# Turning the small matrices of two linear-attention layers by DMA instead of rebuilding them on TensorE

## The chip, the core and the metric

The kernel runs on one core of a Trainium2 chip, in one launch. A core has five instruction streams that matter here: TensorE (PE in the profile; its weight loads are PEld), VectorE (DVE), ScalarE (ACT), GpSimd (POOL) and SyncE (SP), which issues every DMA of this kernel in one queue. The metric is the device time of the core in microseconds; a comparison uses the median of several runs.

## The reference, cut to what matters

Forward and backward pass of four residual layers on x of 2048 tokens by 512 features, bfloat16. Layers 0 and 2 are linear attention with the same weights, layers 1 and 3 gated linear units with the same weights. The outputs are the forward result and the gradients of x and of the five weight matrices.

```
phi = lambda t: jnp.where(t > 0, t + 1, jnp.exp(t)) + 1e-6
pq, pk = phi(q), phi(k)                              # 32 heads of 16
kv = jnp.einsum("bhsd,bhse->bhde", pk, v)            # per head 16x16
z = jnp.einsum("bhsd->bhd", pk)                      # sum of the keys
o = (pq @ kv) / (pq @ z + 1e-6);  return o @ wo
...
x = x + A(layernorm(x)); x = x + B(layernorm(x))     # layers 0, 1
x = x + A(layernorm(x)); x = x + B(layernorm(x))     # layers 2, 3
out, vjp = jax.vjp(f, x, wqkv, wo, w_gate, w_up, w_down)
```

An attention layer thus passes through a few small matrices that every token depends on: kv (128x512 as four block-diagonal 128x128 blocks), z, and kv times wo, called Wp (512x512). The backward pass needs the same things turned, and its own: the gradient of kv (dkv) and its products with the value weights, U and its transpose UT.

## The kernel before, in words

Tokens are worked in eight blocks of 256, each as two halves of 128. Five sweeps go over the blocks, and neighbouring sweeps overlap:

- sweep 1: layernorm of layer 0, keys (`a_k`, k_ps) and the sum G of h times pk (g_acc, g_ps), queries (`a_q`, q_ps);
- first barrier (`a_barrier` of layer 0): kv from G (kv_ps), Wp from kv (wp_ps), z;
- sweep 2: attention output of layer 0 (`a_p2`: den_ps, reciprocal, ya_ps), layernorm, layer 1 (g_ps, u_ps, y_acc of `glu_fwd`), layernorm, keys and queries of layer 2;
- second barrier (`a_barrier` of layer 2);
- sweep 3: attention output of layer 2, layer 3 forward and backward (`glu_both`), and the first half of layer 2's backward pass (`a_b1`: dpn_ps with WpT and Zn, m_ps);
- backward barrier (`a_bbarrier`): dkvT, U (u_ps), UT, dkv;
- sweep 4: the second half of layer 2's backward pass (`a_b2`: dpk_ps with U, dha_ps with UT), layer 1 backward, first half of layer 0's;
- sweep 5: the rest of layer 0, and then `dw`: the weight gradients (dw_ps), which fill the last quarter.

No instruction order is written out by hand. Each function adds pieces to a plan `k.G` (class `Plan`): a piece has a key such as `UT2.1`, its time on TensorE, the keys it follows, the engine steps behind it with their costs, and the buffer tokens it takes and gives. `Plan.run` plays an event model with one queue for each engine and one for DMA ("D"), and issues the instructions in the order in which the model grants them. A piece's rank is the longest path behind it plus an entry of the table `OFFSETS`. On the chip each engine keeps that order, so that an instruction that waits holds all behind it on its engine; SP does so with DMAs too. Model costs decide the order alone, not the time on the chip. Transfers are modelled as megabytes over a rate: `RATE` for plain ones, `TURNED` for DMA transposes.

What the change touches:

- In `a_barrier`, `wpt` computes Wp turned a second time from kv and wo (L739, 16 matmuls of 128 columns for each layer), and `turn` makes kv and Zn (z in blocks, turned) by four TensorE transposes each (L759). Results go from PSUM to SBUF by ACT. Layer 0's WpT is stored to WpT_d and loaded again as WpTl in sweep 4.
- In `a_bbarrier`, `ut` computes UT (L1102, four matmuls of 512 columns for each layer) and `dkv` the untransposed dkv from MTb and woT (L1111, 16 matmuls), beside `dkvT` (L1069) and `u` (L1079).
- In `a_k`, `zsum` adds up the keys (L642): 16 matmuls of one column for every two blocks, into z_ps, for both layers.
- Turns by DMA exist already: rTx from rx in `a_p2` (L861), gT from g in `a_b1` (L1009), both 128x512 from SBUF, and larger ones from HBM (hT, pkT, the dw_sets).

Pools: PSUM has five "mm" buffers, two "acc" and one "tp"; SBUF has six "s1" buffers of 128x512 and seven "w4" of 512x512.

Of the kernel before, what the change touches and what calls it, by code (L numbers as in the profile page):

```python
# [74 lines left out]
class Plan:  # L75
# [11 lines left out]
    RATE, TURNED = 0.27, 0.235  # L87
# [16 lines left out]

    def load(self, key, fn, mb, deps=(), use="", pull=0.0, turn=False):
        self.add(key, fn, 0.0, deps, [("D", mb / (self.TURNED if turn else self.RATE))], use, pull=pull)

    def store(self, key, fn, mb, deps=(), free=""):
        self.add(key, fn, 0.0, deps, [("D", mb / self.RATE, free)], side=True)
# [169 lines left out]
TURN = (6, 1, 1)  # L279
ACCJ, ACCY = 11, 7  # L280
# [8 lines left out]
    DE0:3=-33,4=+11,5=+6,7=+11 DE2:0=-23,1=-155,2=-22 DK0:4=+21 DP0:0=+49,1=-15,2=+49,3=+49,4=-66,7=-5  # L289
    DP2:2=+21,4=+10,5=+30 DT0:+79 DW1:1=-22,2=-1,3=-1,5=-8,6=-49,7=-9 DW3:1=+10,4=-2 E3:0=+1,1=-1 Fg3:11=+20  # L290
    G1:0=-32,1=+1 G11:1=+46,5=-36,6=+40 GS0:3=+14,4=-9,5=-66,6=-362 GS2:6=+63 J1:0=+63 K0:0=-17,2=+93 K2:2=+31
    LB1:2=-23 LB2:7=+3 LB3:2=-24,4=+2 LDH2:6=-3 LDL0:7=+15 LDP0:3=-7,7=-7 LDX0:4=-6 LG3:0=+67
    LN0:1=-208,2=-119,5=-109,6=-19,7=-144 LN2:7=-83 LP2:1=+18 LS1:3=-4,5=-4,6=-4 LX0:3=+16,4=+16 MS0:1=-1,5=-128
    MS2:1=-29 Q0:1=-86,4=-160,6=-53,7=+154 Q2:0=-18,1=-11,2=-12,4=+2 RX2:2=+53,3=-30 S0:-40 SDX1:4=-62 SDX3:0=-92
    SH2:2=-17,4=-11 SHH1:2=-21,4=-21,5=-92 SJ1:+26 SM2:-84 SN0:4=+85,5=-2 SO0:3=-11 SP2:2=-92,3=+50 SPREAD:-142
    SQ0:1=-58 SR0:3=-38,4=-57,5=-38,6=-36,7=-38 SU1:0=-17,6=-41 SU3:2=-14 TG0:1=+2,2=+6,4=-73 TK0:2=+394,5=+132
    TR1:2=+19,5=-7 TR3:4=+32 WT2:0=+41,1=+12 Y1:4=-9 Y33:1=-27,4=-34 YA0:0=-98,6=+10 YA2:1=-31,2=+11 ZE0:3=+36,5=-31
    ZE2:0=+58,1=+61,2=+78,3=+94,4=+173,5=+131,6=+174 ZN2:-46 ZS0:3=+12 ZS2:7=+79 ZZ2:-116
# [7 lines left out]
def kernel(  # L306
# [48 lines left out]
    k.WpT_d = dt_("WpT_d", [P, NDC * D])  # L355
# [69 lines left out]
def build_consts(k, consts):  # L425
# [33 lines left out]
    k.pm = consts.tile([P, 2], F32, name="pm")  # L459
# [51 lines left out]

def layernorm(k, l, b, x_fn, deps, sums=False):
# [4 lines left out]
    def half_sums(j):  # L517
        if j == 0:
            k.h[l, b] = t2(k, f"h{l}", [P, 2, D])
        h, x_t = k.h[l, b], x_fn()  # L520
        col = slice(2 * B + j, 2 * B + j + 1)
        rs, sx = k.rstd[l][:, col], k.sx[l][:, 2 * b + j:2 * b + j + 1]
        q = k.p1.tile([P, 4], F32, name="ln_q", tag="ln_q", bufs=4)
        nc.scalar.activation(h[:, j, :], x_t[:, j, :], ACT.Square, accum_out=q[:, 0:1])
        yield
        nc.gpsimd.tensor_tensor(q[:, 1:3], sx.to_broadcast([P, 2]), k.pm[:], ALU.mult)
        yield
        nc.gpsimd.tensor_scalar(q[:, 0:1], q[:, 0:1], 1.0 / D, EPS_LN, ALU.mult, ALU.add)
        yield
        nc.gpsimd.tensor_scalar(rs, q[:, 1:2], q[:, 2:3], q[:, 0:1], ALU.mult, ALU.add)  # L530
        yield
        nc.gpsimd.tensor_tensor(rs, rs, k.neghalf[:, 0:1], ALU.pow)
        yield
        nc.gpsimd.tensor_tensor(q[:, 3:4], q[:, 1:2], rs, ALU.mult)
        yield
        nc.scalar.activation(h[:, j, :], x_t[:, j, :], ACT.Identity, bias=q[:, 3:4], scale=rs)
        if l in k.rstdh:
            yield
            nc.gpsimd.tensor_scalar(k.rstdh[l][:, col], rs, 0.5, 0.0, ALU.mult, ALU.add)
# [46 lines left out]
def a_k(k, l, b, keep, by_dma=False):  # L586
# [50 lines left out]
    def zsum():  # L637
        ps = tpps(k, [P, NDC], "z_ps", F32)
        for c in range(NDC):
            for i in range(4):  # L640
                bb, j = b - 1 + i // 2, i % 2
                nc.tensor.matmul(ps[:, c:c + 1], lhsT=A.pk[bb][:, j, cslice(c)], rhs=k.ones_col[:],  # L642
                                 start=(i == 0), stop=(i == 3))
        yield
        if b == 1:
            A.z = k.p1.tile([P, NDC], F32, name="z", tag="z", bufs=2)
            nc.vector.tensor_copy(A.z[:], ps[:])
        else:
            nc.vector.tensor_tensor(A.z[:], ps[:], A.z[:], ALU.add)
# [7 lines left out]
    if l == 2 and b in SUMS:  # L657
        gs, prev = SUMS[b]
        for m in range(NDC):
            G.add(f"GS{n}.{m}", lambda m=m: gsum(m, gs, True, True), 2 * len(gs) * C512,  # L660
                  [f"K{l}.{bb}.{j}" for bb in gs for j in range(2)] + [f"GS{l}.{prev}.{m}"] + ([f"<GS{n}.{m - 1}"] if m else []),
                  [("A", 0.59, "-mm") if b == 1 else ("V", 0.69, "-mm")],
                  "+mm" + (" +accf" if b == 1 and m == 0 else " +w4" if b == NBLK - 1 and m == 0 else ""))
    if b % 2 == 1:
        bs = [b - 1, b]
        ks = [f"K{l}.{bb}.{j}" for bb in bs for j in range(2)]
        G.add(f"ZS{n}", zsum, 16 * 0.027, ks + [f"ZS{l}.{b - 2}", f"ZB{l - 2}"], [("V", 0.2, "-tp")], "+tp")
        for bb in bs:
            nb = b if l == 2 and bb not in SUMS else bb
            G.free("-t2", [f"<GS{l}.{nb}.3", f"SH{l}.{bb}", f"TK{l}.{bb}.1"])  # L670
            G.free("-t2", [f"<GS{l}.{nb}.3", f"SPK{l}.{bb}", f"<ZS{n}"])
# [13 lines left out]
def a_barrier(k, l):  # L685
# [42 lines left out]
    G.add(f"KV{l}", kv, 16 * C128, cg + ["WV", f"KT{l - 2}", f"WT{l - 2}.3", f"ZN{l - 2}"], [("V", 0.69, "-mm")], "+mm")  # L728
# [4 lines left out]

    def wpt(m):
        if m == 0:
            A.WpT = w4(k, f"WpT{l}")
        ps = mmps(k, [P, NDC, P], "wpt_ps")
        for c in range(NDC):
            nc.tensor.matmul(ps[:, c, :], lhsT=k.wo[:, c, cslice(m)], rhs=A.kvT[:, c, :], start=True, stop=True)  # L739
        yield  # L740
        nc.scalar.copy(A.WpT[:, m, :], flat(ps[:]))
# [11 lines left out]
    def turn(nm):  # L753
        src = st["zbd"] if nm == "Zn" else A.kvT[:]
        dst = k.consts.tile([P, NDC, P], BF16, name=f"{nm}{l}")
        setattr(A, nm, dst)
        tps = tpps(k, [P, NDC, P], "zn_ps")
        for c in range(NDC):
            nc.tensor.transpose(tps[:, c, :], src[:, c, :], k.ident[:])  # L759
        yield  # L760
        nc.scalar.copy(dst[:], tps[:])
    for m in range(NDC):
        G.add(f"WT{l}.{m}", lambda m=m: wpt(m), 4 * C128, wps + ([f"<WT{l}.{m - 1}"] if m else []), [("A", 0.59, "-mm")],
              "+mm" if m else "+mm +w4")
    if l == 0:
        G.store("SW", lambda: nc.sync.dma_start(out=k.WpT_d[:], in_=flat(A.WpT[:])), 2 * BLK, [f"WT{l}.{m}" for m in range(NDC)], "-w4")
    G.add(f"ZB{l}", zbd, 0.0, [f"ZS{l}.{last}"] + wps, [("V", 0.68, "+s1"), ("V", 0.17)])
    G.add(f"ZN{l}", lambda: turn("Zn"), 4 * C128, [f"ZB{l}"], [("A", 0.59, "-tp")], "+tp -s1")
    G.add(f"KT{l}", lambda: turn("kv"), 4 * C128, wps, [("A", 0.59, "-tp")], "+tp")
# [172 lines left out]
def a_b1(k, l, b, deps):  # L942
# [71 lines left out]
    for hf in range(2):  # L1014
        G.add(f"DP{n}.{hf}", lambda hf=hf: dpn(hf), 8 * C256,
              [f"TG{n}.0", f"TG{n}.1"] + ([f"LP{n}", "WPL0"] if l == 0 else [f"LP{n}"]) + ([f"<DP{n}.0"] if hf else [f"<DP{l}.{b - 1}.1"]) + [f"WT{l}.{m}" for m in range(NDC)],
# [39 lines left out]
def a_bbarrier(k, l):  # L1056
# [41 lines left out]
    def ut(c):  # L1098
        if c == 0:
            A.UT = w4(k, f"UT{l}")  # L1100
        ps = mmps(k, [P, D], "ut_ps")
        nc.tensor.matmul(ps[:], lhsT=st["dkvT"][:, c, :], rhs=k.wvT[:, c, :], start=True, stop=True)  # L1102
        yield
        cp(k, c, A.UT[:, c, :], ps[:])

    def dkv():
        A.dkv = k.consts.tile([P, NDC, P], BF16, name=f"dkv{l}")
        ps = mmps(k, [P, NDC, P], "dkv_ps")
        for c in range(NDC):
            for m in range(NDC):  # L1110
                nc.tensor.matmul(ps[:, c, :], lhsT=A.MTb[:, m, cslice(c)], rhs=k.woT[:, m, cslice(c)],  # L1111
                                 start=(m == 0), stop=(m == NDC - 1))
        yield
        nc.vector.tensor_tensor(A.dkv[:], ps[:], bdm(), ALU.mult)
# [8 lines left out]
    for c in range(NDC):  # L1123
        G.add(f"UT{l}.{c}", lambda c=c: ut(c), C512, [f"<U{l}.3"] + ([f"<UT{l}.{c - 1}"] if c else []), cpost(c, "mm"),
              "+mm" if c else "+mm +w4")
    G.add(f"DKV{l}", dkv, 16 * C128, [f"<U{l}.3"] + ms, [("V", 0.69, "-mm")], "+mm")
    G.free("-w4", [f"SM{l}", f"<DKV{l}", f"<DT{l}"])
    G.free("-s1", [f"<U{l}.3", f"<UT{l}.3"])
# [454 lines left out]
def sweep1(k):  # L1583
# [9 lines left out]
    for b in range(NBLK):  # L1593
# [5 lines left out]
        a_k(k, 0, b, True)  # L1599
# [8 lines left out]
    G.free("-w4", ["<WT2.3", "<WP2.3"])  # L1608
# [3 lines left out]
def sweep2(k):  # L1612
# [26 lines left out]
    G.free("-w4", [f"<YA0.{last}.1"])  # L1639
# [3 lines left out]
def sweep3(k):  # L1643
# [35 lines left out]
    G.free("-w4", [f"<YA2.{last}.1"])  # L1679
# [6 lines left out]
def sweep4(k):  # L1686
# [4 lines left out]
    def wpl():  # L1691
        A0.WpT = w4(k, "WpTl")
        nc.sync.dma_start(out=flat(A0.WpT[:]), in_=k.WpT_d[:])
# [3 lines left out]
    G.load("WPL0", wpl, 2 * BLK, [f"<DP2.{last}.1", "WKT", "SW", "UT2.3"], "+w4")  # L1697
# [17 lines left out]
    G.free("-w4 -w4", ["<UT0.3", "<DKV0"])  # L1715
# [220 lines left out]
```

## Time and profile before

| | |
|---|---|
| runs | median 1094.3 us of 9 (1092.81 to 1096.01) |
| profiled execution | 1092.81 us, its span 1091.0 us |
| matmuls | 7524 |
| DMA | 236.94 MB in 491745 packets, mean 217 GB/s |
| busy share, DVE / ACT / POOL | 59% / 33% / 16% |
| DMA issues | all on SP, one after another |

The span runs from the first to the last instruction; the profiled execution's time has 1.8 us around it. A row's "busy" is the union of the times of its instructions, and matmuls overlap, so that a row's mean is longer than the distance from one matmul to the next. "Idle before" is what the engine waited ahead of an instruction, with what ended the wait. For a DMA, the row on SPq is the time of the issue; the landing comes later.

### The profile page before, as it was taken

The numbers are of one execution on the slowest core, as the hardware profiler recorded it, in microseconds if no ns is written. First come the engines' busy times: TensorE is split into PE (matmuls) and PEld (weight loads), VectorE is DVE, ScalarE is ACT, GpSimd is POOL, SyncE is SP. The second block draws the span as 40 slices with busy tenths as digits, with TensorE's granted clock in tenths as the row PEclk, the third lists the DMA queues.
The fourth block names the chain that finished last, engine by engine and source line by source line (L and its number), as shares of the span: only waits on it lengthen the run. The fifth ranks groups of instructions, "written<-read, shape, count | busy, mean of one in ns | idle before, by whom it ended". The sixth has DMA issues, their size and how long they took to land.

```text
span 1091.0 us, 19982 instructions
## 1 busy us (share of the span) xinstructions
PE 1068.9 (98%) x7524; PEld 700.7 (64%) x7524; DVE 640.2 (59%) x1580; ACT 363.6 (33%) x729; POOL 172.3 (16%) x444
## 2 busy tenths in 40 slices
PE   6989999999999999999999999989999999999998
PEld 3667767667567666676556566656554466666787
DVE  6897776699766886788856667868746000000010
ACT  6675565456343343332244543332111000000010
POOL 4136655305230212000000000000000000000000
PEclk9999999999999999999999999999999999999999
DMA  7748889984988888765979699969999999999960
GB/s 239 246 128 282 233 253 270 280 187 130 227 215 214 207 220 198 203 160 136 277 202 259 210 274 255 273 153 261 238 252 278 239 224 205 232 227 223 198 157 20
DMA packets 491745, 236.94 MB, mean 217 GB/s; under 512 B 317600, under 2 KB 476544, under 8 KB 489600
## 3 DMA queue, kind: packets, MB, share of 16 engines
q1 hardware_dynamic: 491648, 235.66, 85.0%
q8 instruction: 59, 0.97, 0.4%
q14 instruction: 38, 0.31, 0.1%
HBM read 62.46 MB, written 95.72 MB: 145 GB/s over the span
## 4 chain that ended last, share of the span: by engine, by line
PE 74%; DVE 2%; SPq 1%; DMA 1%; issue 0%; ACT 0%; DVEq 0%; ACTq 0%
PE dw_ps L1818 26%; PE dha_ps L1205 8%; PE dh_acc L1336 7%; PE dh_acc L1334 7%; PE dhh_ps L1264 7%; PE g_ps L1264 3%; PE u_ps L1264 3%; PE y_ps L1456 3%; PE dpk_ps L1189 3%; PE m_ps L1036 2%; PE dpn_ps L975 2%; PE ya_ps L901 1%; DMA dw_set<-hh_d 1%; PE gT_ps L483 1%; PE dpn_ps L988 1%; PE q_ps L790 1%
## 5 line engine op out<-in xcount | busy, mean ns | idle before, releaser
L1818 PE MATMUL dw_ps<-dw_set,h 128*128 128x352 bf16 (+2 forms) x1536 | 205.6, 297 | 0.0
L1818 PEld LDWEIGHTS <-h 128*128 128x128 bf16 x1536 | 150.3, 98 | 55.3
L1800 DVE TENSOR_SCALAR dw_o<-dw_ps 128x512 bf16<-128x512 f32 (+3 forms) x33 | 17.6, 540 | 232.0 <-PE dw_ps L1818 226.7
L1336 PE MATMUL dh_acc<-wgT,dg 128*128 128x512 bf16 x352 | 133.4, 379 | 0.2 <-DVE dg L1511 0.2
L1334 PE MATMUL dh_acc<-wuT,du 128*128 128x512 bf16 x352 | 133.4, 379 | 0.0
L1798 ACT ACTIVATE dw_o<-dw_ps 128x512 bf16<-128x512 f32 (+4 forms) x34 | 16.1, 481 | 245.2 <-PE dw_ps L1818 229.7
L1264 PE MATMUL u_ps<-hT,wu 128*128 128x256 bf16 x704 | 92.5, 273 | 0.0
L1264 PE MATMUL g_ps<-hT,wg 128*128 128x256 bf16 x704 | 92.5, 273 | 0.0
L1264 PE MATMUL dhh_ps<-gT,wdT 128*128 128x256 bf16 x704 | 88.4, 273 | 1.3 <-ACT gT L485 1.2
L1143 POOL TENSOR_SCALAR ab<-c 128x2 f32<-128x2 f32 x64 | 20.2, 316 | 410.0 <-DVE lnb_j L1140 409.5
L1264 PEld LDWEIGHTS <-wg 128*128 128x128 bf16 x704 | 68.5, 98 | 21.3
L1818 PE MATMUL dw_ps<-g,dw_set 128*128 128x512 bf16 (+1 forms) x352 | 77.9, 379 | 2.9 <-DMA dw_set<-hh_d 2.9
L1264 PEld LDWEIGHTS <-wdT 128*128 128x128 bf16 x704 | 68.4, 98 | 14.4 <-issue 2.0
L1264 PEld LDWEIGHTS <-wu 128*128 128x128 bf16 x704 | 68.9, 98 | 8.0
L1818 PEld LDWEIGHTS <-dw_set 128*128 128x128 bf16 (+1 forms) x352 | 35.1, 100 | 42.1 <-DMA dw_set<-hh_d 3.4
L1137 ACT ACTIVATE lnb_t<-dha_ps,rstd 128x512 f32<-128x512 f32 x32 | 22.0, 687 | 109.2 <-PE dha_ps L1205 79.0
L1336 PEld LDWEIGHTS <-dg 128*128 128x128 bf16 x352 | 34.4, 98 | 35.1 <-DVE dg L1511 0.5
L1334 PEld LDWEIGHTS <-du 128*128 128x128 bf16 x352 | 34.4, 98 | 34.4
L1389 ACT ACTIVATE th<-g_ps 128x512 f32<-128x512 f32 (+1 forms) x48 | 26.7, 557 | 73.7 <-PE g_ps L1264 54.6
L1295 DVE SCALAR_TENSOR_TENSOR hh<-th,u_ps 128x512 bf16<-128x512 f32 (+1 forms) x48 | 30.3, 638 | 24.2 <-ACT th L1290 17.2
L1509 DVE TENSOR_TENSOR du<-s2tl,dhh 128x512 bf16<-128x512 bf16 (+1 forms) x48 | 18.9, 401 | 41.1 <-ACT dhh L1504 38.3
L1306 PE MATMUL y_acc<-wd,hh 128*128 128x512 bf16 x176 | 42.7, 379 | 0.0
(215 smaller groups left out, 1821.1 us busy)
## 6 DMA issues: line engine op xcount, KB each, us to landing
s2t_d<-s2t SPq DMA_DIRECT2D x8, 1408.0 KB, 6.1
s2tl<-s2t_d SPq DMA_DIRECT2D x8, 1408.0 KB, 7.7
hh_d<-hh SPq DMA_DIRECT2D x16, 640.0 KB, 4.5
du_d<-du SPq DMA_DIRECT2D x80, 128.0 KB, 2.8
dg_d<-dg SPq DMA_DIRECT2D x80, 128.0 KB, 2.9
h_d<-h SPq DMA_DIRECT2D x32, 256.0 KB, 2.6
h<-h_d SPq DMA_DIRECT2D x18, 256.0 KB, 4.4
pk_d<-pk SPq DMA_DIRECT2D x16, 256.0 KB, 3.1
```

What stands on the lines that cost most here:

```text
L975: nc.tensor.matmul(ps[:, c2, :], lhsT=A.WpT[:, m, cslice(c)], rhs=st["gT"](m), start=(c2 + m == 0), stop=False, skip_group_check=True)
L1137: nc.scalar.activation(t[:], dh_ps, ACT.Identity, scale=rs, accum_out=c12[:, 0:1])
L1189: nc.tensor.matmul(ps[:, c2, :], lhsT=A.U[:, m, cslice(2 * hf + c2)], rhs=st["hT"][:, m, :], start=(m == 0), stop=(m == NDC - 1))
L1205: nc.tensor.matmul(ps[:], lhsT=lh[:, c, tslice(j)], rhs=rh[:, c, :], start=(i + c == 0), stop=(i == 2 and c == NDC - 1))
L1264: nc.tensor.matmul(ps[:, i, :], lhsT=w[:, m, fsl(fc)], rhs=rhsT[:, m, :], start=(m == 0), stop=(m == NDC - 1))
L1295: nc.vector.scalar_tensor_tensor(hh, th[:, 0:w], 1.0, flat(up[:])[:, 0:w], ALU.add, ALU.mult)
L1306: nc.tensor.matmul(st["acc"][j][:], lhsT=st["hh"][:, fc, tslice(j)], rhs=k.wd[:, fc, :], start=(fc == 0), stop=(fc == NFC - 1))
L1334: nc.tensor.matmul(acc[j][:], lhsT=du[:, i, tslice(j)], rhs=k.wuT[:, fc, :], start=(fc == 0), stop=False)
L1336: nc.tensor.matmul(acc[j][:], lhsT=dg[:, i, tslice(j)], rhs=k.wgT[:, fc, :], start=False, stop=(fc == NFC - 1))
L1389: nc.scalar.activation(th[:, 0:w], flat(gp[:])[:, 0:w], ACT.Tanh, scale=0.5)
L1456: nc.tensor.matmul(ps[:], lhsT=st["hh"][:, fc, tslice(j)], rhs=k.wd[:, fc, :], start=(fc == 0), stop=(fc == NFC - 1))
L1818: nc.tensor.matmul(ps, lhsT=lhs(s_), rhs=rhs(s_), start=(s_ == 0), stop=(s_ == 31))
```

## The change

- `add_dma_turn` is new: it turns a 512x512 matrix by four DMA transposes of 128x512, SBUF to SBUF. Layer 2's WpT comes from Wp this way, and UT from U in both layers. `wpt` and `ut` are gone.
- Zn, kv and dkv are turned by one DMA transpose each. The TensorE transposes and the dkv matmuls are gone.
- Layer 0's Wp is stored as it is (Wp_d) and turned as it is loaded in sweep 4 (WpTl).
- In layer 2, blocks 0 to 6 of the keys are added up by GpSimd into zf (fp32, one copy and 13 adds of 128x512). At the end `zsum` sums zf over its rows with four fp32 matmuls against a column of ones (k.pm) and adds block 7 with eight bfloat16 matmuls. Layer 0 keeps its 64 matmuls.
- The event model has a faster plain rate with a floor for each issue, and two rates for turned transfers, split at 0.3 MB. `OFFSETS` has new values, so the order changes in many places. `TURN0 = 8` adds an argument that is false for every block.

```diff
-    RATE, TURNED = 0.27, 0.235
+    RATE, ISSUE, TURNED, SETS = 0.3, 0.45, 0.225, 0.22
...
+    def moved(self, mb, turn=False):
+        if turn:
+            return mb / (self.SETS if mb > 0.3 else self.TURNED)
+        return max(mb / self.RATE, self.ISSUE)
...
+def add_dma_turn(k, key, get, make, deps, use="", free=""):
+    st = {}
+    def turn(i):
+        if i == 0:
+            st["t"] = make()
+        k.nc.sync.dma_start_transpose(out=st["t"][:, :, cslice(i)], in_=get(i))
+    for i in range(NDC):
+        k.G.load(f"{key}.{i}", lambda i=i: turn(i), BLK, deps[i] + ([f"~{key}.{i - 1}"] if i else []), "" if i else use, turn=True)
...
+    def zadd(j):
+        pk = A.pk[b][:, j, :]
+        if j == 0 and b == 0:
+            A.zf = k.p1.tile([P, D], F32, name=f"zf{l}", tag="lnf", bufs=BUFS["lnf"])
+            nc.gpsimd.tensor_copy(A.zf[:], pk)
+        else:
+            nc.gpsimd.tensor_tensor(A.zf[:], A.zf[:], pk, ALU.add)
...
         for c in range(NDC):
-            for i in range(4):
-                bb, j = b - 1 + i // 2, i % 2
-                nc.tensor.matmul(ps[:, c:c + 1], lhsT=A.pk[bb][:, j, cslice(c)], rhs=k.ones_col[:],
-                                 start=(i == 0), stop=(i == 3))
+            if l == 2:
+                nc.tensor.matmul(ps[:, c:c + 1], lhsT=A.zf[:, cslice(c)], rhs=k.pm[:, 2:3], start=True, stop=False)
+            for i, t in enumerate(its):
+                nc.tensor.matmul(ps[:, c:c + 1], lhsT=t[:, cslice(c)], rhs=k.ones_col[:],
+                                 start=(l == 0 and i == 0), stop=(i == len(its) - 1))
...
-            nc.tensor.matmul(ps[:, c, :], lhsT=k.wo[:, c, cslice(m)], rhs=A.kvT[:, c, :], start=True, stop=True)
-        nc.scalar.copy(A.WpT[:, m, :], flat(ps[:]))
...
-            nc.tensor.transpose(tps[:, c, :], src[:, c, :], k.ident[:])
-        nc.scalar.copy(dst[:], tps[:])
+        nc.sync.dma_start_transpose(out=dst[:], in_=flat(src))
...
+        G.store("SW", lambda: nc.sync.dma_start(out=k.Wp_d[:].rearrange("(c p) j -> p c j", p=P), in_=A.Wp[:]), 2 * BLK, wps)
+        add_dma_turn(k, f"WT{l}", lambda c: A.Wp[:, c, :], make, [[w] for w in wps], "+w4")
+    G.load(f"ZN{l}", lambda: turn("Zn"), BLK, [f"ZB{l}"], turn=True)
+    G.load(f"KT{l}", lambda: turn("kv"), BLK, [f"KV{l}"], turn=True)
...
-        nc.tensor.matmul(ps[:], lhsT=st["dkvT"][:, c, :], rhs=k.wvT[:, c, :], start=True, stop=True)
-        cp(k, c, A.UT[:, c, :], ps[:])
...
-                nc.tensor.matmul(ps[:, c, :], lhsT=A.MTb[:, m, cslice(c)], rhs=k.woT[:, m, cslice(c)],
-                                 start=(m == 0), stop=(m == NDC - 1))
-        nc.vector.tensor_tensor(A.dkv[:], ps[:], bdm(), ALU.mult)
+        nc.sync.dma_start_transpose(out=A.dkv[:], in_=flat(st["dkvT"]))
...
+    add_dma_turn(k, f"UT{l}", lambda m: A.U[:, m, :], make, [[f"U{l}.{m}"] for m in range(NDC)], "+w4")
+    G.load(f"DKV{l}", dkv, BLK, [f"DT{l}", f"~UT{l}.3"], turn=True)
+    G.free("-s1", [f"<U{l}.3", f"DKV{l}"])
...
-        nc.sync.dma_start(out=flat(A0.WpT[:]), in_=k.WpT_d[:])
+        nc.sync.dma_start_transpose(out=A0.WpT[:], in_=k.Wp_d[:])
```

Lines and shapes in this text are those of the kernel before.

## Prediction

> **What bounds the kernel now.** I read the page's busy times first, then the trace's waits of TensorE, then single rows. From the page:
>
> ```profile
> PE 1068.9 (98%) x7524; PEld 700.7 (64%) x7524; DVE 640.2 (59%) x1580; ACT 363.6 (33%) x729; POOL 172.3 (16%) x444
> PEclk9999999999999999999999999999999999999999
> PE 74%; DVE 2%; SPq 1%; DMA 1%; issue 0%; ACT 0%; DVEq 0%; ACTq 0%
> ```
>
> TensorE (PE) is busy 98% of the span at full granted clock, and the chain that ended last lies on it. But a row's busy time hides pipelining: the mean of a 128-column matmul is 219 ns, yet in the timeline 16 of them (dkv_ps) start at 530.38 and the next group at 531.27.
>
> ```profile
> 528.34 1.05 PE L1079 MATMUL u_ps<-dkvT,wvT 128*128 128x128 bf16 x16 [0.25 <-DVE dkvT L1072]
> 529.23 1.25 PE L1102 MATMUL ut_ps<-wvT,dkvT 128*128 128x512 bf16 x4
> 530.38 1.05 PE L1111 MATMUL dkv_ps<-woT,MTb 128*128 128x128 bf16 x16
> 531.27 3.66 PE L1189 MATMUL dpk_ps<-hT,U 128*128 128x256 bf16 x32
> 534.76 1.03 PE L1205 MATMUL dha_ps<-wkT,dkT 128*128 128x512 bf16 x4
> ...
> 230.11 0.54 PE L642 MATMUL z_ps<-ones_col,pk 128*128 128x1 bf16 x16
> 230.52 1.67 PE L624 MATMUL g_ps<-pk,h 128*128 128x512 bf16 x7
> ```
>
> So one matmul costs its distance to the next start: 56 ns for 128 columns, 109 for 256 (32 in 3.49 us), 216 for 512 (4 in 0.86), 25 for the one-column z_ps (16 in 0.41). All 7,524 matmuls at these paces are 1062.3 us. The span, 1091.0, is this plus 6.7 before the first matmul, about 3 behind the last start, and 19 of gaps. I added up the gaps between starts, stage by stage: 5.8 in the first 50 us, 3.8 from 60 to 73 (first attention barrier), 3.2 from 237 to 291 (second), 2.1 from 527 to 551, 3.1 before the first dw_ps at 734.7; hardly anything elsewhere. The waits of TensorE name what ends the largest:
>
> ```profile
> PE hTk_ps L483 <- ACT h L560: 6.7, 1, 6.7
> PE dw_ps L1818 <- DMA dw_set<-hh_d: 2.9, 1, 2.9
> PE ya_ps L901 <- DVE pnT L889: 1.2, 1, 1.2
> PE dhh_ps L1264 <- ACT gT L485: 1.2, 1, 1.2
> PE ya_ps L901 <- DVE rphiT L894: 1.1, 2, 0.6
> ```
>
> The consequence: work taken off TensorE shortens the run one for one, unless it stood in a gap; and whatever makes TensorE wait is added whole.
>
> **The change, part by part.**
>
> *1. Work off TensorE.* Removed: wpt_ps 32, dkv_ps 32, zn_ps 16, all 128 columns: 80 x 56 ns = 4.5 us. ut_ps 8 x 216 ns = 1.7. Of 128 z_ps, 56 go: 56 x 25 ns = 1.4. Added: four fp32 matmuls z_ps<-pm,zf of one column. No row of the trace is fp32. Low end 25 ns each, as the bf16 ones; high end 0.5 us each, a 512-column matmul's 379 ns plus a weight load's 98. The moving side is one column, but the weights are twice as wide; I take 0.2 each, 0.9 in all with the wait behind POOL (0.1 to 2). Sum: 7.6 - 0.9 = **-6.7** (-5.6 to -7.5). Also gone are 16 evictions of 0.59 us on ACT and 6 of 0.69 on DVE; what they shorten is booked in parts 2 to 4.
>
> *2. First barrier.* I laid the new instruction order out at these paces. Before, the second half of ya_ps of block 0 ends at 64.5 and g_ps starts at 72.41: 7.9 us of layernorm and turn (DVE, ACT, five POOL steps, ACT, PE, ACT), with 4.3 us of matmuls to fill it and 3.8 of gaps in that stage. The new order has kv_ps four us earlier, more q_ps behind it, and 5.8 us of matmuls between the same two points although the wpt_ps filler is gone. With the latency at 7.3, contention being less, about 1.5 us of gap stays, and 0.7 for ya_ps waiting on pnT: 2.2 for 3.8, **-1.6** (-3 to +0.5). SP issues a kv, a Wp store and a Zn more ahead of rTx of block 2; SP is idle from 57.4 to 67.8 here, which hides them.
>
> *3. Second barrier.* Gaps before: 0.3, 0.65, 0.8, 1.5. Now 2.7 us of matmuls stand between r_ps and ya_ps of block 0 (before 2.0), 2.0 for block 1 (1.5), 29 between den_ps and ya_ps of block 3. I leave 1.0: **-2.2** (-3.2 to +1.5). WpT's four turns stand on SP where it is idle (239.1 to 243.3 and 245.3 to 251.6), and WpT's reader dpn_ps comes 108 us of matmuls later. kv and Zn are read later still.
>
> *4. UT of layer 2: the new wait on TensorE.* In matmul time (6.7 plus paces, no gaps) the new order has u_ps end at 509.1; then y_ps 2.4, dpk_ps 3.5 and eight dha_ps 1.7 stand before the first dha_ps<-UT at 516.7, which waits for a DMA. The four turns stand on SP behind two gT, s2tl, MT_d and four 256-KB transposes, with dqT in their middle. The nearest rows, a turn of the same 128x512 shape from SBUF, and the queue as it ran before:
>
> ```profile
> L861 SPq DMA_TRANSPOSE rTx<-rx x24: 1188/1218/2442, 68.2 to 422.4; - x24
> DMA to landing us min/median/max: 2.4/2.5/5.5
> ...
> 517.25 0.53 SPq L1478 DMA_DIRECT2D s2tl<-s2t_d  x1
> 517.88 1.60 SPq L1173 DMA_TRANSPOSE hT<-h_d  x1
> 519.57 3.57 SPq L1173 DMA_TRANSPOSE pkT<-pk_d  x1
> ...
> 525.86 2.55 SPq L1173 DMA_TRANSPOSE pkT<-pk_d  x1
> ```
>
> (Issue min/median/max in ns, landing from the issue; then start, us.) From s2tl to the last pkT the queue runs without a pause for 11.2 us, data behind it: s2tl's pass for 4.8 us before the first hT's do. In the new order gT goes 5.8 us behind the last dh_acc, as before (508.9 to 514.7), at 496.4; s2tl at 499.0, its data until 503.8; MT_d at 503.3, when MTb is evicted, until 505.7; four transposes at 1.27 until 510.8; UT 2 x 1.2, dqT 0.9, UT 2 x 1.2: 516.5, and 1.0 for the rest of the landing: 517.5 against 516.7, with the whole program of TensorE behind it. If the data keep up with SP, 516.2 and no wait. Before it, dkT needs dz, five small DVE steps behind the last junk: before 6.4 us after zn's matmuls, now some 5, at 513, and four dkT steps bring it to 515.5 against 515.0. Together 1.5; dhh_ps behind gT waits 0.9 for ACT's copy. 2.4 for 2.1: **+0.3** (-1.2 to +4).
>
> Here the Trainium skill speaks against the change. "VectorE: DVE Perf Modes", in "The three transpose paths", puts a 128x128 bf16 turn at 390 ns on TensorE and 1309 ns through the DMA, and its rules choose TensorE where a PSUM target will do. Both differ from this trace: four blocks take 4 x 56 ns of TensorE's time, and rTx brings four blocks in 1.2 us of queue, 0.3 each. By the page UT's four would be 16 x 1.3 = 21 us (an estimate) in place of 4.8, and part 4 some +16. The measured row is of this very shape; it decides.
>
> *5. Layer 0's turn and the dw start.* WpTl turned on load costs SP some 2.8 us (wqT, the same size: 2.83) for 0.34, and dkv 1.2, where SP idled 6.5 us between 543.7 and 550.3; dpn_ps reads it at 567.0 of matmul time, over 45 us behind the issue. UT of layer 0 has 19.7 us of matmuls behind u_ps; ahead of it stands one dw_set of 4.4: covered by some 8. The first dw_set stands on SP as before, matmuls ahead of dw_ps are 9.55 us for 9.1: **-0.5** of its 3.1.
>
> *6. POOL.* One copy and 13 adds, 128x512, between 100 and 235 us. No two-input add of that size is in the trace; nearest s2t (one input) 678 ns; the skill's "GPSIMD Engine Reference", "Elementwise", gives 2.6 cycles per element for two inputs, by which 512 are an estimated 1.1 us. I take 1.1: 15 us on an engine that is busy 63 of 135 us there. Queued behind an add are the layernorm's small steps, for which hT and then g_ps wait; five adds in a row hold them 5.5 us. TensorE had no gap there, so slack is unseen: 0 to 4, with DVE slowed through a shared port included; I take **+1.0**, also for dkvT's s1 buffer, now held into the last stage, and the new transfer rates, which move only order.
>
> Sum: -6.7 - 1.6 - 2.2 + 0.3 - 0.5 + 1.0 = **-9.7**. The profiled execution took 1092.8 (span 1091.0 and 1.8 around), the fastest of nine, 1.5 under the median; the same step from the median 1094.3 gives **1084.6**.
>
> **Rivals.**
> - *Only the work goes.* The 4.3 us that parts 2, 3 and 5 take off the gaps are latency that the new order does not hide, or come back elsewhere. For it: two of these stages lost matmuls that filled gaps. Then -6.7 + 0.3 + 1.0 = -5.4, 1088.9; about 1092.5 with the high end of 4 or 6. Against it: the counted cover is longer at each place.
> - *Slower: UT2 lands late.* If SBUF turns run near the page's price, or queue behind s2tl and four transposes for longer than the row says, dha_ps stands still. The forecast holds under 1 us of this wait; from 10.5 the gain is gone, from 12.7 it is slower by over 0.2%. By the page's price 16 more: 1100.6. Against it: 24 rTx of a median 2.5 us, at most 5.5.
> - *The work isn't the bound*, so nothing moves: against it stand 98% and the sparse gaps.
>
> **How the numbers follow.** 0.2%, 2.2 us, is about what a measurement can tell. Forecast (1081 to 1087.5) 0.55; only the work (1087.5 to 1092) 0.24; the same with a further wait, within 0.2%, 0.06; UT2 slower 0.10; better than 1080.5, 0.05. Faster 0.84, same 0.06, slower 0.10. The range 1080.5 to 1093 leaves out UT2, the tail below, and the upper half of "same".
>
> **What would show it.** 7,384 matmuls (140 fewer); wpt_ps, zn_ps, ut_ps, dkv_ps gone; PE busy some 7 to 8 us less. z_ps<-pm under 0.5 us each. A wait of dha_ps for the DMA of UT near 526, under 2 us: above 10 the second rival holds, none means the queue kept up with SP. UT issues near 1.2 us. ya_ps and hT_ps waits at the barriers smaller than 7.0 in all; if not, the first rival. zf adds near 1.1 us, no wait of g_ps on hT in 100 to 235.

## The result, and the profile after

The changed kernel takes 1090.3 us (median of 10 runs, 1088.9 to 1093.0) where the kernel before took 1094.4 on the same chip (31 runs): a ratio of 0.9964, 95% interval 0.9955 to 0.9974, or 4 us less. The forecast was 9.7 us less. A second set of runs on another chip gave 0.9964 again (0.9952 to 0.9977). Direction and range were right; less than half of the gain came.

The profiled execution took 1093.4 us, the slowest of the eleven executions measured, so its span must not be held against the one before. These lines of its page answer to the first ones shown of before:

```profile
span 1091.7 us, 19746 instructions
PE 1066.3 (98%) x7388; PEld 695.3 (64%) x7388; DVE 641.0 (59%) x1571; ACT 356.9 (33%) x713; POOL 185.7 (17%) x459
```

TensorE has 136 matmul records fewer (140 by the diff; the four fp32 ones count twice). Its waits, largest first behind the 7.0 us at the start (us in all, times, longest):

```profile
...
PE dw_ps L1831 <- DMA dw_set<-hh_d: 2.5, 1, 2.5
PE ya_ps L926 <- DVE pk L600: 1.7, 1, 1.7
...
PE hT_ps L490 <- ACT h L555: 1.3, 1, 1.3
PE ya_ps L926 <- DVE rphiT L919: 1.3, 2, 1.1
PE gT_ps L490 <- ACT gT L492: 1.2, 1, 1.2
...
PE dpn_ps L1000 <- ACT gT L492: 0.8, 1, 0.8
PE dhh_ps L1277 <- ACT gT L492: 0.7, 1, 0.7
PE u_ps L1104 <- ACT U L711: 0.5, 1, 0.5
...
PE dha_ps L1218 <- DMA UT<-U: 0.3, 1, 0.3
```

Of the waits shown of before, dw_ps and the first barrier's are still here in much the same size. A gap is named here by the moment at which it begins. New are ya_ps behind pk at 154 us, u_ps and y_ps behind U's eviction, a second gT, dpn_ps behind gT, and UT. A wait counts from the end of the last matmul, which is modelled; the gap between starts, less the pace of the matmul ahead of it, is up to 0.2 longer. I added those gaps up by stage, for two profiles of the changed kernel (the second is of the run called "the same, again" below), with the fp32 matmuls at their own pace, as work:

| stage, us | before | after | after, again | forecast | found |
|---|---|---|---|---|---|
| up to 50 | 5.9 | 5.0 | 5.8 | none | -0.9 to -0.1 |
| first barrier, 50 to 75 | 4.1 | 4.5 | 4.5 | -1.6 | +0.4 |
| GpSimd's sums, 75 to 230 | 0 | 2.9 | 2.3 | +1.0 | +2.3 to +2.9 |
| second barrier, 230 to 300 | 3.4 | 1.5 | 1.5 | -2.2 | -1.9 |
| 300 to 500 | 0.3 | 0.8 | 0.2 | none | -0.1 to +0.5 |
| backward barrier, 500 to 560 | 2.4 | 5.8 | 5.9 | +0.3 | +3.5 |
| dw start and last stage, from 720 | 3.1 | 5.7 | 5.0 | -0.5 | +1.9 to +2.6 |
| all stages | 19.2 | 26.2 | 25.3 | -3.0 | +6.1 to +7.0 |

(The expectations below count a one-column matmul at 27 ns and the fp32 ones likewise, hence their 18.7, 25.6 and 26.5.) In the column "after", 1.5 us of the backward barrier and 1.6 of the last stage are no waits but a TensorE clock at half speed for 3.4 us (last section). Work less by 6.7 and gaps more by 6.1 nearly cancel, as the spans do (1090.7 for the second profile, 1091.0). The medians still differ by 4, because the first profile of before was a lucky execution, 1.6 us under its median, and the second profile of the changed kernel comes from a chip on which both kernels take some 2 to 3 us more (medians 1097.1 and 1092.6). Of single profiles only the gaps that hang on engines may be compared; the larger ones come back to 0.02 us from one profile to the next, but for one at 547 (last section). Those that hang on transfers do not.

### The profile page after: what moved, and what is told of

It is laid out like the page before. It is cut to its first block, busy times and chain, and to the rows that moved or that the text cites. A ratio compares the mean times of both kernels' runs of the same rounds, so it can differ in the third digit from the quotient of the medians.

```text
span 1091.7 us, 19746 instructions
## 1 busy us (share of the span) xinstructions
PE 1066.3 (98%) x7388; PEld 695.3 (64%) x7388; DVE 641.0 (59%) x1571; ACT 356.9 (33%) x713; POOL 185.7 (17%) x459
```

## The experiments

All edits but the two unchanged kernels are made in the changed kernel, its order of instructions kept on every engine; only the instructions named come, go or move to another engine or buffer.

| run | ratio to before | 95% interval |
|---|---|---|
| changed kernel | 0.9964 | 0.9955 to 0.9974 |
| the same, again | 0.9964 | 0.9952 to 0.9977 |
| key sums on TensorE | 0.9957 | 0.9942 to 0.9972 |
| key sums added twice | 1.0007 | 0.9994 to 1.0019 |
| U evicted on ScalarE | 0.9965 | 0.9953 to 0.9978 |
| Wp evicted on ScalarE | 0.9961 | 0.9948 to 0.9975 |
| u_ps in other banks | 0.9976 | 0.9964 to 0.9988 |
| ya_ps in other banks | 0.9969 | 0.9952 to 0.9986 |
| five edits together | 0.9968 | 0.9953 to 0.9983 |
| UT of layer 2 on TensorE | 0.9959 | 0.9945 to 0.9973 |
| UT of layer 0, dkv on TensorE | 0.9965 | 0.9951 to 0.9979 |
| all UT and dkv on TensorE | 0.9968 | 0.9955 to 0.9982 |
| only kv, Zn, Wp by DMA | 0.9971 | 0.9955 to 0.9988 |
| kv, Zn, Wp on TensorE | 1.0037 | 1.0021 to 1.0054 |
| only the new order | 1.0030 | 1.0011 to 1.0049 |

**Key sums of layer 2 back on TensorE.** Four groups of 16 matmuls over two blocks each, as before; no zf.

```diff
-            nc.gpsimd.tensor_tensor(A.zf[:], A.zf[:], pk, ALU.add)
+        if j == 1 and b % 2:
+            A.zg = zsum([b - 1, b])
```

> The changed kernel, its order kept, with the key sums of the second layer back on TensorE: 56 bf16 one-column matmuls more, the 14 GpSimd operations and the eight fp32 matmul passes gone. TensorE's work is +0.5 us (56 x 25 ns less 0.9). Theory: the adds stretch VectorE's two-input and fast one-input operations that run beside them (a rphiT of 0.24 us took 1.24 at 154.0) and cost TensorE 2 to 3 us of gaps between 85 and 157; then those gaps (0.42 at 85.9, 0.54 at 119.9, 1.89 at 154.3) shrink to under 0.5 in all in that window's last part, rphiT's operations at 150 to 156 go back to 0.24 to 0.68 each, and the time is 1.0 to 2.0 us under the changed kernel, about 1088.8. Rival: the adds hide, and the gap at 154 belongs to the order (VectorE late whatever GpSimd does); then the gap stays and the time is 0.5 over the changed kernel, 1090.8.

The timeline of GpSimd and VectorE in the changed kernel (start, us, engine, line):

```profile
150.91 4.19 POOL L662 TENSOR_TENSOR zf<-zf,pk 128x512 f32<-128x512 f32 x3 [1.70 <-DVE pk L600]
151.82 0.64 DVE L900 TENSOR_SCALAR rphiT<-pqT 128x512 bf16<-128x512 bf16 x1
152.72 1.37 DVE L902 TENSOR_TENSOR rphiT<-rphiT,rTx 128x512 bf16<-128x512 bf16 x1
154.01 1.24 DVE L900 TENSOR_SCALAR rphiT<-pqT 128x512 bf16<-128x512 bf16 x1
155.71 0.68 DVE L600 SCALAR_TENSOR_TENSOR pk<-k_ps,phi_e 128x512 bf16<-128x512 f32 x1
```

and VectorE's with the sums on TensorE:

```profile
150.94 0.29 DVE L897 TENSOR_SCALAR rphiT<-pqT 128x512 bf16<-128x512 bf16 x1
151.47 0.42 DVE L899 TENSOR_TENSOR rphiT<-rphiT,rTx 128x512 bf16<-128x512 bf16 x1
151.81 0.29 DVE L897 TENSOR_SCALAR rphiT<-pqT 128x512 bf16<-128x512 bf16 x1
```

Beside the three adds, operations of 0.29 and 0.42 us take 0.64 to 1.37, each ending some 0.15 to 0.3 us behind the end of an add; pk, which reads PSUM and one SBUF operand, keeps its 0.68. ya_ps then waits for pk, the gap of 1.9 at 154, and it is gone in this run. But a gap of 1.25 opens at 221 (hTk_ps behind z, on VectorE, L675). The time is 0.8 us lower than the changed kernel's by the ratios, inside both intervals: the mechanism is shown, the gain is not.

**Key sums added twice.** Each add is done again, and the final column is 0.5 instead of 1.

```diff
+        nc.gpsimd.tensor_tensor(A.zf[:], A.zf[:], pk, ALU.add)
```

> The changed kernel with each GpSimd operation of the key sums followed by a second add (28 operations, 15 us more of GpSimd between 148 and 226; the last matmuls take half the sum, so nothing else changes). Same order on every other engine. Theory (the adds slow VectorE and so TensorE): the stretch doubles and the time goes up by 1.5 to 4 us over the changed kernel, 1092 to 1094, with VectorE's rphiT and pnT operations near 150 to 158 longer. Rival (the adds hide): same time within 0.5 us. Second rival (the adds only hold the layernorm's small GpSimd steps): longer waits of g_ps on hT, VectorE's durations as they were.

Slower than the changed kernel by 0.0043, 4.7 us, more than the theory's 1.5 to 4; the gap at 154 grew to 2.8, and 0.4, 0.6 and 1.5 opened at 170, 179 and 226, the last of them g_ps waiting for pk of VectorE. So the adds do not hide; and VectorE's rphiT operations near 152 took up to 1.37 us here too, so that it is not the small steps alone, as the second rival had it. 14 more adds cost over twice the 1.9 us of the gap at 154, which suggests that there is a little cover and that the change had used it up.

**U evicted on ScalarE alone.**

```diff
-        cp(k, m, A.U[:, m, :], flat(ps[:]))
+        cp(k, m if l == 0 else 0, A.U[:, m, :], flat(ps[:]))
```

> The changed kernel with all four evictions of u_ps of layer 2 on ScalarE, which sat idle 11 us before them, in place of two on VectorE behind dqT and junk. Theory: u_ps and the next y_ps stand still 0.6 us each because U's evictions hold the PSUM banks, and dkvT, junk, dqT and two U evictions in a row on VectorE set when banks come free; then the gaps at 524.0 and 525.0 fall from 1.2 to 0.3 to 0.8 in all, UT's turns are issued about 0.5 earlier, and the wait of dha_ps for UT (0.3 to 0.5) goes: 0.5 to 1.3 us under the changed kernel. Rival: banks are not the limit but dz and dkT behind VectorE; then u_ps's gaps move but dha_ps starts at the same time, no change within 0.3.

Neither: u_ps and y_ps still waited 0.61 us each. In the timeline of the changed kernel they wait for ScalarE's own evictions, of the first and the third u_ps; moving the other two off VectorE touches neither.

```profile
523.58 0.61 PE L1104 MATMUL u_ps<-dkvT,wvT 128*128 128x128 bf16 x8
...
524.64 0.61 PE L1104 MATMUL u_ps<-dkvT,wvT 128*128 128x128 bf16 x8 [0.45 <-ACT U L711]
...
525.70 2.53 PE L1469 MATMUL y_ps<-wd,hh 128*128 128x512 bf16 x11 [0.45 <-ACT U L711]
```

**u_ps in other PSUM banks.** The third and fourth u_ps use the two "acc" buffers.

```diff
-        ps = mmps(k, [P, NDC, P], "u_ps")
+        ps = accps(k, "u_ps")[:].rearrange("p (c j) -> p c j", c=NDC) if l == 2 and m > 1 else mmps(k, [P, NDC, P], "u_ps")
```

> The changed kernel, its order kept, with the third and fourth u_ps of layer 2 in the two PSUM banks of dh_acc, which stand empty there, and not in the five that all other matmuls share. Theory: u_ps and y_ps stand still 0.61 us each for a bank that the first U evictions hold; then both gaps go, dpk_ps starts 1.2 us earlier, and dha_ps may meet UT's transfer instead: 0.5 to 1.2 us under the changed kernel. Rival: the two gaps come from dkvT's late eviction, not from banks; then they stay, no change within 0.3.

Both gaps went, so they were banks. But the gap of TensorE ahead of the first dha_ps<-UT grew to 1.70, against 0.47 and 0.86 in the two unedited profiles, by most or all of the 1.2 that had gone:

```profile
PE dha_ps L1218 <- DMA UT<-U: 1.5, 1, 1.5
```

The first dha_ps<-UT began at 533.97 here and at 533.76 in both unedited profiles. The transfer sets that moment; u_ps had only stood in its shadow. No gain (0.9976).

**Wp of layer 0 evicted on ScalarE alone**, and **ya_ps in other banks** (the first four of layer 0 in the "acc" buffers), two edits on the first barrier:

```diff
-        cp(k, c, A.Wp[:, c, :], ps[:])
+        cp(k, c if l == 2 else 0, A.Wp[:, c, :], ps[:])
```

> The changed kernel with all four evictions of wp_ps of layer 0 on ScalarE: 1.3 us taken off VectorE near 55 to 57, 1.2 added to ScalarE, which is busy 4.6 of the 10 us from 52 to 62. Theory: VectorE, busy 27.45 of the 28 us from 47 to 75 (26.85 before the change), is what sets the pace of the first barrier, so taking matmuls off TensorE there only widened gaps; then the first g_ps of the next layer comes 0.7 to 1.3 us earlier and the time falls by as much. Rival: the latency of the layernorm chain sets it and VectorE only fills; then g_ps comes at the same time, within 0.3.

```diff
-        ps = mmps(k, [P, D], "ya_ps")
+        ps = accps(k, "ya_ps") if l == 0 and b < 2 else mmps(k, [P, D], "ya_ps")
```

> The changed kernel, its order kept, with the four ya_ps of the first two blocks of layer 0 in the two PSUM banks of g_acc, which stand empty by then. Theory A (a bank): ya_ps of block 0 waits 1.25 us for the bank that r_ps holds until VectorE's rphiT is done; then that gap falls to about 0.3, xa, the layernorm and hT come 0.9 earlier, and so does g_ps. Theory B (VectorE sets the pace of this barrier, busy 27.45 of 28 us): ya_ps starts earlier but xa stands in VectorE's queue behind the same work, the gap moves to hT_ps, and g_ps comes at the same time, within 0.3.

The first freed 1.05 us of VectorE, and the four largest gaps of TensorE in this barrier stayed within 0.01 us. Busy time from 47 to 75 us (us, then PE, PEld, DVE, ACT, POOL, clock, DMA share, GB/s), the unedited kernel first, then this one:

```profile
47.00:75.00 28.00, 24.52 (x241) 18.30 (x240) 27.41 (x74) 16.46 (x32) 5.65 (x16) 1.00 0.50 153
```

```profile
47.00:75.00 28.00, 24.52 (x241) 18.31 (x240) 26.36 (x72) 17.34 (x34) 5.96 (x17) 1.00 0.48 146
```

VectorE then stood idle at one place:

```profile
58.54 0.29 DVE L598 TENSOR_SCALAR phi_e<-phi_e 128x512 bf16<-128x512 bf16 x1 [0.91 <-ACT phi_e L596]
```

ScalarE was not late there. Its phi_e started 5.25 us behind kv_ps, as in the unedited kernel, where it had waited for q_ps of TensorE (unedited first, then this run):

```profile
58.19 0.60 ACT L596 ACTIVATE phi_e<-q_ps 128x512 bf16<-128x512 f32 x1 [0.85 <-PE q_ps L815]
```

```profile
57.88 0.63 ACT L596 ACTIVATE phi_e<-q_ps 128x512 bf16<-128x512 f32 x1
```

VectorE's next step, pnT, needs r_ps of TensorE and began 6.34 us behind kv_ps in both. So the edit freed VectorE at a place where TensorE comes next.

In the second run ya_ps began 1.25 us sooner behind kv_ps, so its wait was one for a bank; and its result waited: from pnT to xa VectorE took 4.24 us in the run of all five edits and 4.23 in the unedited one. The stage's gaps were 4.5 in both. The first g_ps came 18.84 us behind kv_ps, 18.86 unedited and 18.86 with the Wp edit. From pnT at 59 us on, VectorE has no wait up to 74 us in either run (17.94 us busy of the 18 from 56 to 74 in the unedited second profile), and ScalarE's rx, which stands ahead of the last h and hT before g_ps, waits 0.7 us for its pqT. So by the timelines VectorE paces the barrier from 59 us on. No run took work off VectorE behind that moment; the Wp edit, taken alone, ended as its rival had it.

**Five edits together**: sums on TensorE, U and Wp on ScalarE, both bank edits.

> The changed kernel with five edits together: layer 2's key sums on TensorE, all of U's and layer 0's Wp evictions on ScalarE, the third and fourth u_ps and the first four ya_ps in the accumulators' PSUM banks. Theory (banks and the shared port hold TensorE back): 2 to 3 us under the changed kernel, gaps of 1.89 at 154, 1.2 at u_ps and about 1 in the first barrier gone, ratio to the kernel before near 0.994. Rival (each removed gap comes back at the next one): within 1 us of the changed kernel.

The rival's case. The gaps of 1.9 at 154 and 1.2 at u_ps were gone; 1.25 at 222, 1.0 at UT, 2.7 at dw_ps and 1.0 at 881 (a dw_set) were there.

**The changed kernel again**, and **the kernel before again**, unedited:

> The changed kernel as it is, for a second profile and for its time on the same chip as the three edits below it. Theory: the gaps that hang on engines come back to within 0.02 us (1.25 and 1.48 in the first barrier, 1.89 at 154, 0.61 and 0.61 at u_ps, 1.34 and 0.84 at gT, 0.94 before dpn_ps of layer 0), and those that hang on transfers vary (the first dw_set 2.6, UT 0.5). Rival: the engine gaps vary too, and the first profile was an odd one.

It held: 1.25, 1.48, 1.89, 0.61, 0.61, 1.34, 0.84 and 0.93 came back, while the first dw_set's gap was 1.2 after 2.6, UT's 0.86 after 0.47, and one of 1.4 at 880 and one of 1.3 at 547 (gT behind g) were new.

> The kernel before the change as it is, for a second profile. Its first profiled execution was the fastest of the nine shown (1092.8 for a median of 1094.3), with 18.7 us of gaps between matmul starts. Theory: an ordinary execution has about 1.5 us more, 20 to 21, so the changed kernel's 25.6 to 26.5 are some 5 to 6 more and not 7 to 8. Rival: 18.7 again, and the median's excess is spread or outside.

1099.1 us, on a chip whose median is 1096.2: more than an ordinary execution this time, its span 5.9 us over the first. It has the same engine gaps as the first profile and three that the first had not, 0.85, 0.65 and 0.70 at 370, 382 and 431 us, besides a longer one (3.7) for the first dw_set:

```profile
PE dw_ps L1818 <- DMA dw_set<-hh_d: 3.5, 1, 3.5
...
PE ya_ps L901 <- DVE dqT L998: 0.7, 1, 0.7
...
PE q_ps L790 <- DMA hTq<-h_d: 0.5, 1, 0.5
```

96 of its matmul records are missing, so only gaps of 0.25 us or more can be counted: 19.0 us, where the first profile has 15.6 by the same rule. An ordinary execution of before lies between the two; how many us of gaps it has is not measured. Against this profile two rows of the table find nothing: it has 2.2 us of gaps from 300 to 500, and in the last stage 4.5 and another 1.5 of half clock.

**UT of layer 2 on TensorE**, four 512-column matmuls in the place of the turns:

```diff
+        ps = mmps(k, [P, D], "ut_ps")
+        nc.tensor.matmul(ps[:], lhsT=st["dkvT"][:, c, :], rhs=k.wvT[:, c, :], start=True, stop=True)
+        nc.scalar.copy(A.UT[:, c, :], ps[:])
```

> The changed kernel, its order kept, with UT of layer 2 built by four 512-column matmuls on TensorE (0.86 us) and ScalarE evictions, as it was before; four turns of 1.2 us leave the SP queue at 526 to 532. Theory (the new wait is real and of its forecast size): dha_ps's wait for UT (0.5 to 1.7 us in the profiles) goes, 0.86 comes back: within 0.7 us of the changed kernel, either way. Rival (the turns also hold back what stands behind them on SP: hl, s2tl, h1l and so gT and dhh_ps): the gap before the second gT near 548 goes too, 1 to 2 us under the changed kernel.

The wait for UT went, and the later wait of gT too, the rival's sign but without its gain; 0.86 us of work came, and in this profile waits for transfers stood elsewhere (hTq at 244, 2.3; a dw_set at 880, 2.0). The ratio did not move.

**UT of layer 0 and both dkv on TensorE**, the same four matmuls for layer 0, and

```diff
-        nc.sync.dma_start_transpose(out=A.dkv[:], in_=flat(st["dkvT"]))
+        for c in range(NDC):
+            nc.tensor.transpose(tps[:, c, :], st["dkvT"][:, c, :], k.ident[:])
+        nc.scalar.copy(A.dkv[:], tps[:])
```

> The changed kernel, its order kept, with UT of layer 0 on TensorE again (four 512-column matmuls, 0.86 us) and dkv of both layers turned by four 128-column transposes each (0.45 in all): 1.3 us of TensorE more, six turns fewer on SP, five of them behind 745. Theory (the last 350 us are set by SP and the transfers as much as by TensorE, so that matmuls taken from there come back as gaps): gaps behind 745 shrink by about as much, time within 0.5 us of the changed kernel. Rival (TensorE alone sets the last stage): 1.3 us slower than the changed kernel.

Again the same ratio, and here the profiles show where the work went. Behind 745 us the eleven profiles in which layer 0's UT and dkv are turned by DMA have 0.4 to 3.0 us of gaps of 0.25 us or more, most of them behind transfers, 1.6 on average; this run has none, the three below that have both on TensorE 0.6, none and 0.5, the two profiles of before none and 0.8. 1.1 us of matmuls taken from that stage came back as waits of about that size.

**All UT and dkv on TensorE**, both edits:

> The changed kernel, its order kept, with both UT on TensorE and both dkv turned there (2.2 us of TensorE more, ten turns fewer on SP): of the change, the key sums and the turns of kv, Zn and Wp are left. Theory (what was taken off TensorE in the backward barriers came back as waits): within 0.7 us of the changed kernel. Rival (one for one): 2.2 us slower, half of the change's gain gone, ratio to the kernel before about 0.9984.

Nearer the theory: 0.4 us over the changed kernel by the ratios, 2.2 was the rival's.

**Only kv, Zn and Wp by DMA**: this, and the key sums on TensorE.

> The changed kernel, its order kept, with the key sums, both UT and both dkv on TensorE (2.7 us of TensorE more than the changed kernel): only the turns of kv, Zn and Wp by DMA are left of the change, with the new order. Theory (the parts undone one by one moved nothing, so their sum doesn't either): within 0.7 us of the changed kernel, ratio to the kernel before near 0.9965. Rival (each part gives a few tenths below what one run can show): 1.5 to 2.7 us slower, ratio 0.998 to 0.999.

0.8 us over the changed kernel. Taken alone none of the five runs that bring matmuls back from the sums, UT or dkv excludes one-for-one, since each interval is 1.5 us wide to either side and the changed kernel's own 1.0. But one for one all five would lie 0.5 to 2.7 us above the changed kernel, by the matmuls that each brings back; each lies 1.2 to 1.9 below its own mark. (Three of them share their runs of before, and all are held against the same ratio of the changed kernel, so they are not five independent readings.)

**kv, Zn and Wp on TensorE**, and **only the new order** (this and the edits of the run above):

```diff
+        for m in range(NDC):
+            nc.tensor.transpose(tps[:, m, :], A.Wp[:, c, cslice(m)], k.ident[:])
+        nc.scalar.copy(dst, tps[:])
```

> The other half: the changed kernel, its order kept, with kv, Zn and Wp of both layers turned on TensorE, 48 transposes of 128 columns (2.7 us) and 12 evictions on ScalarE, in the accumulators' PSUM banks; key sums, UT and dkv stay as changed. The turned Wp of layer 0 is made and not used (its stored copy is still turned on load). Theory (these 48 stood in barriers that VectorE and latencies pace, so they filled gaps): at most 1 us slower than the changed kernel. Rival (these are the part of the change that pays): 2.5 to 3.5 us slower, ratio to the kernel before 0.999.

> The order of the changed kernel with nearly the work of the kernel before: key sums, kv, Zn, Wp, UT and dkv all on TensorE (dkv by 8 transposes instead of 32 matmuls, so 1.3 us less than before; Wp of layer 0 as in the run above). Theory A (the new order carries the gain, the work little): within 1.5 us of the changed kernel, ratio 0.996 to 0.998. Theory B (the work carries it): the ratio is 0.9988 or more, what the missing 24 matmuls leave.

The first is 8 us slower than the changed kernel for 2.7 us of work; the second is 3.3 us slower than the kernel before, with 1.3 us less work than that. TensorE's timeline with the transposes in shows why, in the first barrier and then in the second:

```profile
60.07 0.38 PE L791 MATMUL wpt_ps<-ident,Wp 128*128 128x128 bf16 x4 [0.45 <-ACT Zn L792]
60.69 0.38 PE L791 MATMUL wpt_ps<-ident,Wp 128*128 128x128 bf16 x4 [0.23 <-ACT Zn L792]
```

```profile
250.98 1.03 PE L831 MATMUL q_ps<-hTq,wq 128*128 128x256 bf16 x8 [1.16 <-ACT dhh L1445]
```

The first two wait for the eviction of the transposes ahead of them (the unused copy goes into Zn's buffer, hence the name), the third for ScalarE, which has 12 evictions more. The way from the first matmul to the first g_ps is 1.9 us longer than in the unedited second profile, from there to kv of layer 2 1.2, from there to dkvT 4.5. Both runs give the sign of Theory B, or of the rival, and more than its size. In this order the turns of kv, Zn and Wp carry what there is to gain; and the order without them is worse than the old one. That 8 us is no measure of the change: these transposes stand where the changed kernel issues a transfer, and not, as before, where TensorE was idle. The turned load of layer 0's Wp stood in all these runs; its share is not measured.

No version was found that beats the changed kernel by more than the intervals.

## Why the prediction was right in direction and wrong in size

The step that failed is the one from work to time. TensorE's work fell as forecast, by 6.7 us; its gaps were to shrink by 3.0 and grew by some 2.6. They stand where the working had put nothing or too little: behind VectorE's full queue (part 2), PSUM banks, UT and ScalarE's copies for gT (part 4), and the adds beside VectorE (part 6). The adds and the banks are shown by edits; VectorE's queue and gT are read from the timelines.

*Part 1, the work: -6.7, the count right, its worth wrong.* The four fp32 matmuls show as two each:

```profile
L669 PE MATMUL z_ps<-pm,zf x8: 167/250/250, 233.3 to 234.1; 128*128 128x1 f32 x8
```

From one start to the next it is 0.11 us (0.03 for the first), 0.22 for a matmul: 0.9 in all, as taken. But "work taken off TensorE shortens the run one for one, unless it stood in a gap" was then booked at full price everywhere, though UT and dkv, 3.5 of the 7.6 removed, came from the backward barriers and the last stage, where a transfer is next in line. Brought back at 2.2 (dkv by transposes), they cost 0.4, within the intervals nothing.

*Part 2, first barrier: -1.6 forecast, +0.4 found.* It set a latency of 7.3 us against the matmuls that could fill it. The latency is not a constant: inside it, the steps of the layernorm stand in VectorE's queue, which was nearly full before the change (26.85 of 28 us, in the page's DVE row hidden behind an average of 59%) and was busy for 27.4 after it; the line of before:

```profile
47.00:75.00 28.00, 24.95 (x232) 18.37 (x230) 26.85 (x71) 18.33 (x36) 6.39 (x21) 1.00 0.39 122
```

More matmuls ahead of a full VectorE do not shorten the stage; those moved there, q_ps, bring it work of its own. That is read from the timelines: of the two edits, the one of ya_ps fits it, and the one of Wp freed VectorE too early to try it.

*Part 3, second barrier: -2.2 forecast, -1.9 found.* Right: 0.26, 0.40 and 0.79 stand there now, where 0.3, 0.65, 0.8 and 1.5 stood.

*Part 4, the backward barrier: +0.3 forecast, +3.5 found.* The new wait was sized right: dha_ps waits 0.5 to 0.9 for UT, 0.8 was forecast, UT's issues are 1.22 us where 1.2 was taken. (The sum in the working was wrong: the 0.5 for dkT comes first and would have shifted the 0.8, so that the two make 0.8 and not 1.5. The wait for dkT did not come.)

```profile
L526 SPq DMA_TRANSPOSE UT<-U x8: 1190/1224/2047, 526.2 to 761.7; - x8
```

What failed is the list of what TensorE needs: data and engines were followed, PSUM banks and the second gT were not. u_ps and y_ps wait 1.2 us for banks (before, u_ps alone 0.4, for dkvT), gT and dhh_ps 2.2 behind ScalarE's copies (0.9 forecast, 1.3 before), and after that either gT another 1.3 behind g, or the clock below. The bank wait cost nothing by itself, as its edit shows: UT was behind it. Of the waits of gT no run tells what taking them away would give. The "UT2 lands late" rival did not come; the measured row was the right one against the Trainium skill's price for a DMA turn.

*Part 5: -0.5 forecast, +1.9 to +2.6 found against the first profile of before, nothing against the second.* The first dw_set's gap did shrink, from 3.1 and 3.7 in two profiles of before to 1.2 to 3.3 in the eleven with the turns, 2.2 on average. Missed were dpn_ps behind gT, 0.93 in every profile of the new order, and the waits behind 745 us. The cover of 8 us counted for layer 0's turns was real for UT itself; what the turns took away, by the profiles above, was slack of the transfers behind 745 us; which of the turns did it is open.

*Part 6: +1.0 forecast, 2.3 to 2.9 found, of which 1.9 is shown to be the adds'.* An add takes 1.157 us alone, 1.1 was taken. The queue of small steps that I named did not matter; VectorE's operations beside an add did. I took the port for a slowing. The Trainium skill's "SBUF — State Buffer", "Who interferes with whom", states it harder: the shared pair is an exclusive lock for a whole instruction, taken by a VectorE instruction with two SBUF inputs or in a two-port mode. By the rule each of the three operations near 152 waits for the rest of one add, up to 1.16 us; the rows (0.64, 1.37 and 1.24) agree, as does pk's unchanged 0.68; pnT, begun at 152.38, 0.01 us ahead of the second add, kept its 0.41, and that add took 1.42. That one stretch gives some 2 us of VectorE, which is the gap.

*The sum.* From the medians and the work, an ordinary execution has 6.7 - 4.1, or about 2.6 us more gaps than an ordinary one of before (worked out, not seen): 5.6 above the forecast, which is the whole miss. The first rival, "only the work goes" (1088.9, to 1092.5), described it best, and half for its stated reason: the second barrier's gaps did go, the first's did not, and more came elsewhere.

*A step in the setting up.* The forecast carried a single profile over to the median by adding 1.5. The first profile of before had 19.2 us of gaps, and the second shows waits for transfers it had not; I compared gap by gap with a lucky execution.

## What to carry to other kernels

Before booking matmuls taken off a busy TensorE, ask at each place what stands next in line: a second engine with a full queue there, a PSUM bank, a transfer. Look at busy time in a window of the stage itself, not at the run's average; and where two limits lie within a microsecond of each other, removing one shows only the other. An operation moved to an idle GpSimd can be paid on VectorE: here those that read SBUF alone took up to 1.37 us for 0.42 beside an add.

## What the runs showed of the hardware that I had not expected

*The clock.* Two profiles of one kernel, TensorE from 545 to 548 us (busy, matmuls, granted clock, DMA share, GB/s), after a stretch of 3 us with 1.16 us of work in both:

```profile
545.00:548.00 3.00, 2.99 (x15) 0.52 1.10 210
```

```profile
545.00:548.00 3.00, 1.91 (x16) 1.00 1.06 222
```

In the first, 14 dhh_ps matmuls started 0.213 us apart instead of 0.109, 1.5 us in all; in the second the clock stayed and TensorE waited 1.3 for g instead, and the next gT_ps started at 548.37 and 548.10. The same happened at 736 us. The clock record of the profiles has such stretches, between the start and the end, in thirteen of the seventeen (two in the first of these), each 3.41 us long and behind waits of TensorE (at 247, 545 to 553 or 733 to 743 us). The Trainium skill's "TensorE: Matmul & The Clock Gate", "What's actually happening", puts the gate on a free-running window of about 3.4 us; the length agrees, and the chance of it fits, though our idle time was 1.8 us within 3 and no window was wholly idle. In the times it does not show: the ten other executions had a clock of 1.000 (six, mean 1090.8 us) or 0.998 (four, mean 1090.5).

*GpSimd's adds slow down too*: 1.40, 1.42 and 1.22 us for the three beside VectorE's operations, 1.15 to 1.16 for those alone.
